# Two token groups computed together, weight block by weight block, at the start of a convolution and gated MLP kernel

## The chip, the cores and the metric

The kernel runs on one core of a Trainium2 chip. The metric is the device time of one execution in microseconds (us); lower is better. Engines are named as in the profile: PE is TensorE, DVE is VectorE, ACT is ScalarE, POOL is GpSimd, SP is the queue that issues the DMAs.

## The reference

`x` is 4 x 4096 x 192. A softmax over 7 taps per token and head gives weights, and each token becomes the weighted sum of itself and the six tokens before it, head by head (8 heads of 24 channels). The 16384 rows then go through a gated MLP with 1536 inner columns:

```python
w = softmax(weight_gen, axis=-1)                        # (B, S, 8, 7)
out = np.einsum('bshk,bskhg->bshg', w, x_unfolded)      # 7 taps
x = out.reshape(B * S, 192)
g = x @ w_gate                                          # 192 x 1536
silu = g * (1.0 / (1.0 + np.exp(-g)))
val = x @ w_val
y = (silu * val) @ w_out                                # 1536 x 192
```

The weights come as 64-bit floats; the kernel turns them into 32-bit ones itself.

## The kernel before

The 128 tiles of 128 tokens are worked on in 32 groups of four (`NG`, `JG`). Each group goes through 12 blocks of the inner dimension (`NF`); one group with one block is a step. A step is: the first half of the "up" products (`up_first`: 12 matmuls, the 64 left channels and the low rows of the 128 others), the second half (`up_second`: 6 matmuls), silu on ACT (`silu`), the product `hi` or `h` of silu and value on DVE (`gated`), and two steps later the "down" products with `w_out` (`down`), in four parts, three of them between the two halves of a step and one behind them (at a group's first block two and two).

Matmul operands are split into a high and a low part to keep precision: `x` and the up weights always; `h` and `w_out` too (`hi`, `lo`, `wo`), except in the first `PLAIN` groups, whose down products take plain 32-bit operands (`wo32`). A group that is split needs a `hi` copy on ACT and a `lo` subtraction on DVE in each step.

Two halves of a sum run in different rows of the array at once. That the second half does not overtake the first is kept by a relay: `told(ins)` puts an empty instruction on POOL that waits for a matmul, and `behind(ins, nop)` makes a later matmul wait for that instruction. It stands in POOL's queue in program order.

While group 0 runs, the weight blocks are converted (`weight_ops`), each in four pieces: `exponent` (DVE `e`, ACT `e` and `sign`, POOL `sign`), `mantissa_high` and `mantissa_low` (DVE `m` twice; the second also fetches the raw block four places ahead), and `value32` (DVE `w`, then ACT `wb_hi`, `wa_hi` and `wo`, POOL `wb_lo` and `wa_lo`). `wo32` is split into `wo` later (ACT and POOL).

The order of the work is written by hand. The loop at the end takes one step per pass; `todo[i]` holds the extra operations of step i, and `spread` lays a list evenly over some steps. In `gated`, `between()` takes one operation off that list. For a plain group all of them are issued ahead of `hi`; for the others one between `h` and `lo`, the rest behind.

The taps: group 0 has its seven products made by DVE one by one, copied in part by ACT, and added and turned by TensorE in one (`summed_turn`: 8 matmuls with the identity per tap, two `xatt` buffers). Group 1 has its products made by DVE and, three of them, by POOL (`aside`), added by DVE, and turned by 16 matmuls (`turn`). Later groups are added by DVE and turned by DVE and DMA (`turn_ops`). A group's taps are worked on during the steps of the group before.

Of the kernel before, what the change touches and what calls it, by code (L numbers as in the profile page):

```python
# [18 lines left out]
def dynconv_glu_kernel(  # L19
# [41 lines left out]
    LEAD1 = 1  # L61
    EXP1 = 16
    LOAD1 = 1
    WO = 9

    PLAIN = 1
    MOVED = 2

    HELPED = (0, 3)
    ASIDE = max(HELPED)  # L70
# [153 lines left out]
    def attention_ops(g):  # L224
        cx, cw = chunk_of(xcuts, g), chunk_of(wcuts, g)
        jx, jw = g * JG - xcuts[cx][0], g * JG - wcuts[cw][0]
        helped = HELPED[g] if g < len(HELPED) else 0
# [10 lines left out]
        if g == 0:  # L238
            return mul
# [12 lines left out]
        def aside(k):  # L252
            def go():
                tmp[k] = att.tile([P, JG, D], F32, tag="aside", name="aside", bufs=ASIDE)
                mul(nc.gpsimd, k, tmp[k])

            return go

        def add(k):
            def go():  # L260
                a = xatt[g][:, :, 0:D]
                nc.vector.tensor_tensor(out=a, in0=a, in1=tmp.pop(k), op=ALU.add)  # L262
                if g < MOVED and k == last:
                    a = xatt[g]
                    nc.scalar.activation(out=a[:, :, D:], in_=a[:, :, P:D], func=AF.Copy)

            return go

        ops = [first, product(1)]
        for k in range(2, K - helped):  # L270
            ops += [product(k), add(k - 1)]
        ops += [add(k) for k in range(K - helped - 1, last + 1)]
        return [aside(k) for k in range(K - helped, K)], ops
# [15 lines left out]
    def summed_turn(mul):  # L289

        ps = [ps_up.tile([P, NC], F32, tag="up", name="tr") for _ in range(2)]

        def tap(k):
            def go():
                a = att.tile([P, JG, 2 * P], F32, tag="xatt", name="xatt")
                mul(nc.vector, k, a[:, :, 0:D])
                nc.scalar.activation(out=a[:, :, D:], in_=a[:, :, P:D], func=AF.Copy)
                for half in range(2):
                    for t in range(JG):
                        nc.tensor.matmul(  # L300
                            ps[half][:, t * P : (t + 1) * P],
                            a[:, t, half * P : (half + 1) * P],
                            ident,
                            start=(k == 0 and t == 0),
                            stop=(k == K - 1 and t == JG - 1),
                        )

            return go

        return ps, [tap(k) for k in range(K)]  # L310

    def turn(g, ps, nop):

        places = ((1, LOW), (0, HIGH)) if nop else ((0, LOW), (1, HIGH))
        made = [
            nc.tensor.transpose(
                ps[half][:, t * P + r.start : t * P + r.stop],
                xatt[g][r, t, half * P : (half + 1) * P],
                ident[r, r],
            )  # L320
            for t in range(JG)
            for half, r in places
        ]
        if nop:
            behind(made[0], nop)
            return None
        return told(made[-1])

# [3 lines left out]
    def turn_ops(g):  # L332
# [3 lines left out]
        def blocks():  # L336
            cut = att.tile([P, JG, D], F32, tag="aside", name="cut", bufs=ASIDE)
# [204 lines left out]

    def down(g, f, pair, second):

# [4 lines left out]
        if opens:  # L549
            for t in ts:  # L550
                acc[t] = ps_dn.tile([P, 2 * D], F32, tag=f"dn{t}", name=f"dn{t}")
        order = ts if (f + second) % 2 == 0 else ts[::-1]
        tiles = [(t, r, slice(t * P, (t + 1) * P)) for t, r in zip(order, (LOW, HIGH))]
        if lo is None:
            made = [
                nc.tensor.matmul(  # L556
                    acc[t][:, 0:D], hi[r, cs], wo32[r, f], start=opens, stop=closes
# [3 lines left out]
        else:  # L561
            made = [
                nc.tensor.matmul(  # L563
                    acc[t],
# [5 lines left out]
                for t, r, cs in tiles  # L570
            ] + [
                nc.tensor.matmul(  # L572
                    acc[t][:, 0:D], lo[r, cs], wo[r, f, 0], start=False, stop=closes
# [6 lines left out]
        behind(made[0], half_done.pop(pair))  # L580
        if f < NF - 1:
            return
# [3 lines left out]
        n = D if lo is None else 2 * D  # L586
        for t in ts:
            nc.scalar.activation(out=osb[:, t, 0:n], in_=acc[t][:, 0:n], func=AF.Copy)  # L588
# [3 lines left out]
        if lo is not None:  # L592
            a = osb[:, t0:t1]
            nc.vector.tensor_tensor(
                out=a[:, :, 0:D], in0=a[:, :, 0:D], in1=a[:, :, D:], op=ALU.add
            )
        if g < MOVED:
            nc.sync.dma_start(
                out=outr[:, g * JG + t0 : g * JG + t1], in_=osb[:, t0:t1, 0:D]
            )  # L600
            return
# [9 lines left out]
    turned = {}  # L611
# [7 lines left out]
    with tc.manual_schedule():  # L619
# [32 lines left out]
        later = after[3:]  # L652
        loads = load_x(1) + load_taps(1)
# [6 lines left out]
        todo[0] += later[:3]  # L660
        spread(loads, LOAD1, LOAD1 + 7)
        spread(later[3:], NF - LEAD2 - 2, NF - LEAD2)
        spread(
            [lambda f=f: split(wo[:, f, 0], wo[:, f, 1], wo32[:, f]) for f in range(NF)],
            WO,
            NF + LAG - 1,
        )
# [10 lines left out]
        for g in range(1, NG):  # L678
            s0 = (g - 1) * NF - {1: LEAD1, 2: LEAD2}.get(g, LEAD)
            c = first_x.get(g)  # L680
            if c and c + 1 < len(xcuts):
                todo.setdefault(s0, []).append(lambda c=c: load_x(c + 1)[0]())
            asides, rest = attention_ops(g)
            spread(asides, max(s0, 0), s0 + NF - 4)
            spread(rest, max(s0, 0), s0 + NF - 3)
            if g < MOVED:
                turned[s0 + NF - 2] = g
                continue
            moves, halves = turn_ops(g)
            at = s0 + NF - 3  # L690
# [3 lines left out]
        steps = [(g, f) for g in range(NG) for f in range(NF)]  # L694
        for i in range(len(steps) + LAG + 1):
            ops = todo.pop(i, [])
            to_turn = turned.get(i)
            if i < len(steps):
                g, f = steps[i]
                sums, nop = up_first(g, f)  # L700
                if i in exps:
                    exps[i]()
            late = []
            if i > LAG:
                late = [(*steps[i - LAG - 1], 1, True)]
            if i > LAG and not to_turn:
                down(*late.pop())
            if to_turn:
                ps = [ps_up.tile([P, NC], F32, tag="up", name="tr") for _ in range(2)]
                turned_nop = turn(to_turn, ps, None)  # L710
            if LAG <= i < len(steps) + LAG:
                s = steps[i - LAG]
                late += [(*s, 0, False), (*s, 1, False), (*s, 0, True)]
                if not to_turn:
                    down(*late.pop(0))
                    if s[1]:
                        down(*late.pop(0))
                    else:
                        late.reverse()
# [7 lines left out]
            if to_turn:  # L727
                turn(to_turn, ps, turned_nop)
# [8 lines left out]
            if to_turn:  # L737
                for op in split_ops(to_turn, ps):
                    op()
# [35 lines left out]
```

## Time and profile before

| | |
|---|---|
| median of 3 runs | 1312.7 us (1311.3 to 1313.1) |
| profiled execution, its own time | 1312.98 us |
| its span | 1311.2 us |
| mean granted TensorE clock | 0.990 |
| PE busy | 1270.9 us, 97% |
| DVE busy | 1023.8 us, 78% |
| ACT busy | 594.3 us, 45% |
| POOL busy | 61.2 us, 5% |

The span runs from the first to the last instruction of the program. The busy share is an average: POOL has all its work in the first 103 us, in which the weights are converted, and DVE and PE differ between that stretch and the rest.

### The profile page before, as it was taken

How to read it: one execution, taken by the hardware profiler on the slowest of the kernel's cores; microseconds unless marked ns; L12 is line 12 of the kernel's file. 1: busy time of each engine (PE TensorE's matmuls, PEld its weight loads, DVE VectorE, ACT ScalarE, POOL GpSimd, SP SyncE). 2: the span in 40 equal slices, each digit the busy share in tenths (PEclk: the TensorE clock that was granted, in tenths of full speed). 3: DMA queues.
4: the chain of work that ended last, by engine and by line, in shares of the span. 5: the costliest groups of instructions: out<-in, count | busy, mean ns of one | idle time of the engine just before them, and what ended most of it. 6: DMA issues, size and time to landing. Idle time of an engine off the chain costs nothing.

```text
span 1311.2 us, 31268 instructions
## 1 busy us (share of the span) xinstructions
PE 1270.9 (97%) x13184; PEld 1242.9 (95%) x13184; DVE 1023.8 (78%) x1413; ACT 594.3 (45%) x1049; POOL 61.2 (5%) x62
## 2 busy tenths in 40 slices
PE   5689999999999999999999999999999999999997
PEld 5578899999999999999999999999999999999997
DVE  6978888777887777788777788877778877777843
ACT  5444444454444445444444544444454444444443
POOL 4750000000000000000000000000000000000000
PEclk9789999999999999999999999999999999999999
DMA  6511121212112121211212111221211212111010
GB/s 175 153 47 40 48 72 42 71 42 84 43 33 84 29 84 42 76 33 51 84 29 84 42 36 61 59 71 42 84 41 26 72 39 74 42 42 39 17 40 13
DMA packets 64149, 74.88 MB, mean 57 GB/s; under 512 B 6924, under 2 KB 53516, under 8 KB 62216
## 3 DMA queue, kind: packets, MB, share of 16 engines
q1 hardware_dynamic: 64008, 72.89, 20.1%
q8 instruction: 103, 1.69, 0.5%
q14 instruction: 38, 0.31, 0.1%
HBM read 48.48 MB, written 24.38 MB: 56 GB/s over the span
## 4 chain that ended last, share of the span: by engine, by line
PE 87%; DVE 6%; ACT 2%; DMA 2%; issue 1%; SPq 0%; POOL 0%; ACTq 0%; DVEq 0%; POOLq 0%
PE up L511 23%; PE up L499 22%; PE dn L563 21%; PE up L502 18%; PE dn L572 2%; DVE h L533 1%; DMA xt<-in_x_dram 1%; DVE prod L234 1%; PE tr L300 1%; DVE lo L536 1%; PE dn L556 1%; ACT sg L519 1%; ACT L519 0%; ACT L186 0%; DMA raw<-in_moe_w_gate_dram 0%
## 5 line engine op out<-in xcount | busy, mean ns | idle before, releaser
L563 PE MATMUL dn<-wo,hi 64*128 64x384 f32 x2976 | 578.8, 344 | 0.8 <-ACT osb L588 0.4
L572 PE MATMUL dn<-wo,lo 64*128 64x192 f32 x2976 | 512.2, 249 | 0.3 <-DVE lo L536 0.3
L563 PEld LDWEIGHTS dn<-wo,hi 64*128 64x128 f32 x2976 | 477.4, 184 | 6.9 <-ACT osb L588 2.3
L572 PEld LDWEIGHTS dn<-wo,lo 64*128 64x128 f32 x2976 | 456.4, 186 | 1.8 <-DVE lo L536 0.5
L534 ACT ACTIVATE hi<-h 128x512 fp32r<-128x512 f32 x372 | 235.3, 633 | 377.7 <-DVE h L533 377.7
L533 DVE TENSOR_TENSOR h<-up,sg 128x512 f32<-128x512 f32 x372 | 256.0, 688 | 181.5 <-ACT sg L519 181.3
L519 ACT ACTIVATE sg<-up 128x512 f32<-128x512 f32 x384 | 228.5, 595 | 302.4 <-PE up L511 295.4
L536 DVE TENSOR_TENSOR lo<-h,hi 128x512 fp32r<-128x512 f32 x372 | 254.7, 685 | 83.1 <-ACT hi L534 83.1
L499 PE MATMUL up<-xhi,wb_hi 64*128 64x512 f32 x768 | 223.7, 418 | 8.1 <-DVE hi L528 5.9
L511 PE MATMUL up<-xhi,wa_hi 64*128 64x512 f32 x768 | 218.9, 419 | 10.5 <-POOLq L282 10.4
L499 PE MATMUL up<-xlo,wb_hi 64*128 64x512 f32 x768 | 211.5, 392 | 1.5 <-DVE xlo L384 1.5
L499 PE MATMUL up<-xhi,wb_lo 64*128 64x512 f32 x768 | 211.4, 394 | 0.0
L502 PE MATMUL up<-xhi,wa_hi 64*128 64x512 f32 x768 | 209.9, 391 | 0.2 <-ACT xhi L377 0.2
L502 PE MATMUL up<-xhi,wa_lo 64*128 64x512 f32 x768 | 209.6, 390 | 0.0
L502 PE MATMUL up<-xlo,wa_hi 64*128 64x512 f32 x768 | 208.8, 388 | 0.3 <-DVE xlo L384 0.3
L511 PE MATMUL up<-xhi,wa_lo 64*128 64x512 f32 x768 | 208.2, 391 | 0.0
L511 PE MATMUL up<-xlo,wa_hi 64*128 64x512 f32 x768 | 207.4, 389 | 0.0
L234 DVE TENSOR_TENSOR prod<-xt,wt 128x768 f32<-128x768 f32 x183 | 176.0, 962 | 0.2
L262 DVE TENSOR_TENSOR xatt<-xatt,prod 128x768 f32<-128x768 f32 x183 | 176.1, 962 | 0.0
L499 PEld LDWEIGHTS up<-xhi,wb_hi 64*128 64x128 f32 x768 | 128.6, 185 | 13.0 <-DVE hi L528 7.4
L511 PEld LDWEIGHTS up<-xhi,wa_hi 64*128 64x128 f32 x768 | 127.2, 185 | 13.1 <-POOLq L282 13.1
L502 PEld LDWEIGHTS up<-xhi,wa_hi 64*128 64x128 f32 x768 | 128.4, 185 | 3.1 <-ACT xhi L377 0.7
(60 smaller groups left out, 1306.0 us busy)
## 6 DMA issues: line engine op xcount, KB each, us to landing
xt<-in_x_dram SPq DMA_DIRECT2D x14, 1344.0 KB, 6.8
turned<-cut SPq DMA_DIRECT2D x120, 96.0 KB, 2.0
out_dram<-osb SPq DMA_DIRECT2D x116, 96.0 KB, 1.9
t<-turned SPq DMA_DIRECT2D x60, 128.0 KB, 2.6
t<-turned SPq DMA_DIRECT2D x30, 256.0 KB, 3.0
raw<-in_moe_w_out_dram SPq DMA_DIRECT2D x12, 192.0 KB, 2.7
wt<-in_weight_gen_dram SPq DMA_DIRECT2D x3, 672.0 KB, 4.4
raw<-in_moe_w_gate_dram SPq DMA_DIRECT2D x12, 128.0 KB, 2.2
```

Of the source, the lines that this page charges most:

```text
L234: engine.tensor_tensor(out=into.rearrange("p t (h i) -> p t h i", h=H), in0=src, in1=w, op=ALU.mult)
L262: nc.vector.tensor_tensor(out=a, in0=a, in1=tmp.pop(k), op=ALU.add)
L300: nc.tensor.matmul(ps[half][:, t * P : (t + 1) * P], a[:, t, half * P : (half + 1) * P], ident, start=(k == 0 and t == 0), stop=(k == K - ...
L499: nc.tensor.matmul(ps, w[r, fs], m[r], start=(n == 0), stop=False)
L502: ins = nc.tensor.matmul(sums[i], w[r, i, fs], m[r], start=False, stop=False)
L511: ins = nc.tensor.matmul(sums[i], w[r, i, fs], m[r], start=False, stop=(n == len(full) - 1))
L519: nc.scalar.activation(out=sg, in_=sums[0], func=AF.Silu)
L533: nc.vector.tensor_tensor(out=h, in0=sums[1], in1=sg, op=ALU.mult)
L534: nc.scalar.activation(out=hi, in_=h, func=AF.Copy)
L536: nc.vector.tensor_tensor(out=lo, in0=h, in1=hi.bitcast(F32), op=ALU.subtract)
L563: nc.tensor.matmul(acc[t], hi[r, cs], wo[r, f].rearrange("p a d -> p (a d)"), start=opens, stop=False,)
L572: nc.tensor.matmul(acc[t][:, 0:D], lo[r, cs], wo[r, f, 0], start=False, stop=closes)
```

## The change

Groups 0 and 1 are both plain now (`PLAIN = 2`) and are computed together. A list `steps` gives the order: four steps of group 0 (`HEAD`), then in turn one of group 1 and one of group 0, four blocks ahead, and at the end four of group 1. Each weight block is therefore used by two groups while the conversion goes on, and its pieces are laid by the step in which group 0 needs it (`due`). In the first four steps all extra operations stand ahead of `hi`; in the other plain steps one does and the rest stand behind.

Group 1's taps are made like those of group 0, by `summed_turn`, during steps 0 to 3, in the two PSUM banks that group 1's down products take later. The POOL products, the sums on DVE and `turn` are gone. The down sums of a plain group take two banks, two tiles in each, and are copied out by two ACT instructions. The softmax of the first taps stands wholly ahead of step 0. Group 2's taps begin at step 5. The splits of `wo32` follow group 0's blocks, the first six of them at step 10.

```diff
-    PLAIN = 1
+    PLAIN = 2
     MOVED = 2
+    HEAD = 4
...
-        if g == 0:
+        if g < MOVED:
             return mul
...
+        if g == 0:
+            ps = [ps_up.tile([P, NC], F32, tag="up", name="tr") for _ in range(2)]
+        else:
+            ps = [ps_dn.tile([P, NC], F32, tag=f"dn{2 + n}", name=f"tr{n}") for n in range(2)]
...
         if g < PLAIN:
-            while between():
+            while between() and g == 0 and f < HEAD:
                 pass
...
+            if pair == 0:
+                behind(made[0], half_done.pop(0))
+                behind(made[0], half_done.pop(1))
...
-        for op in after[:3]:
+        for op in after[:6]:
             op()
-        ps, taps = summed_turn(attention_ops(0))
+        ps, taps = summed_turn(0)
         meanwhile = w0 + w1[:2]
-        for op in taps[:2]:
+        for op in taps[:2] + after[6:]:
             op()
...
+        steps = [(0, f) for f in range(HEAD)]
+        for f in range(NF - HEAD):
+            steps += [(1, f), (0, f + HEAD)]
+        steps += [(1, f) for f in range(NF - HEAD, NF)]
+        steps += [(g, f) for g in range(2, NG) for f in range(NF)]
...
-        for i in range(NF):
-            ops = todo.setdefault(i, [])
-            for f, part in ((i + 2, 3), (i + 3, 1), (i + 4, 0), (i + 3, 2)):
-                if f < NF:
-                    ops.append(convert[f][part])
+        ps1, taps1 = summed_turn(1)
+        due = [steps.index((0, f)) for f in range(NF)]
+        for f in range(2, NF):
+            for part, ahead in ((3, 2), (1, 3), (0, 4), (2, 3)):
+                if (f, part) not in ((2, 1), (2, 2), (2, 0), (3, 0)):
+                    todo.setdefault(max(due[f] - ahead, 0), []).append(convert[f][part])
+        spread(taps1, 0, HEAD - 1)
+        spread(split_ops(1, ps1), HEAD - 1, HEAD)
+        spread(load_x(1) + load_taps(1), LOAD1, LOAD1 + 7)
+        for f in range(NF):
+            todo.setdefault(max(due[f] + 3, HEAD + 6), []).append(
+                lambda f=f: split(wo[:, f, 0], wo[:, f, 1], wo32[:, f])
+            )
...
-        for g in range(1, NG):
-            s0 = (g - 1) * NF - {1: LEAD1, 2: LEAD2}.get(g, LEAD)
+        for g in range(2, NG):
+            s0 = (g - 1) * NF - (LEAD if g > 2 else NF - HEAD - 1)
```

How it moves instructions, at the three places that the prediction speaks of. First PE, behind the first step (`up` is what a step writes, `tr` the tap sums, `xatt` a tap). Before, the second half of step 0 is followed by step 1:

```order
L511 MATMUL up<-xhi,wa_hi 128x512 x2
L511 MATMUL up<-xlo,wa_hi 128x512 x2
L511 MATMUL up<-xhi,wa_lo 128x512 x2
L499 MATMUL up<-xhi,wb_hi 128x512 x2
L499 MATMUL up<-xlo,wb_hi 128x512 x2
L499 MATMUL up<-xhi,wb_lo 128x512 x2
```

Now three taps of group 1 stand between them (two rows each), and two more behind each of steps 1 and 2:

```order
L483 MATMUL up<-xhi,wa_hi 128x512 x2
L483 MATMUL up<-xlo,wa_hi 128x512 x2
L483 MATMUL up<-xhi,wa_lo 128x512 x2
L289 MATMUL tr_307<-ident,xatt 128x128 x4
L289 MATMUL tr_308<-ident,xatt 128x128 x4
L289 MATMUL tr_307<-ident,xatt 128x128 x4
L289 MATMUL tr_308<-ident,xatt 128x128 x4
L289 MATMUL tr_307<-ident,xatt 128x128 x4
L289 MATMUL tr_308<-ident,xatt 128x128 x4
L471 MATMUL up<-xhi,wb_hi 128x512 x2
```

PE's queue is in order, so step 1 stands behind the third tap. Second ACT, in steps 0 to 2 (`sg` is silu, `xatt` the copy that a tap needs). Before:

```order
L519 ACTIVATE sg<-up 128x512
L412 ACTIVATE wb_hi<-w 128x128
L412 ACTIVATE wa_hi<-w 128x2x128
L476 ACTIVATE wo_95<-w 128x192
L431 ACTIVATE e<-e,exp_bias 128x576
L433 ACTIVATE sign<-raw 128x576
L519 ACTIVATE sg<-up 128x512
```

Now:

```order
L286 ACTIVATE xatt<-xatt 128x4x64 x3
L491 ACTIVATE sg<-up 128x512
L384 ACTIVATE wb_hi<-w 128x128
L384 ACTIVATE wa_hi<-w 128x2x128
L448 ACTIVATE wo_95<-w 128x192
L403 ACTIVATE e<-e,exp_bias 128x576
L405 ACTIVATE sign<-raw 128x576
L286 ACTIVATE xatt<-xatt 128x4x64 x2
L491 ACTIVATE sg<-up 128x512
L286 ACTIVATE xatt<-xatt 128x4x64 x2
```

The copies of the fourth and fifth tap stand behind silu of step 1 and the five pieces of a weight block. Third DVE, a step in the middle of the conversion (`hi` is the product of the step; `e`, `m` and `w` are pieces of weight blocks). Before, all pieces stand ahead of `hi`:

```order
L462 SCALAR_TENSOR_TENSOR w<-m,sign 128x576
L439 TENSOR_SCALAR m<-raw 128x576
L422 TENSOR_SCALAR e<-raw 128x576
L449 SCALAR_TENSOR_TENSOR m<-raw,m 128x576
L262 TENSOR_TENSOR xatt<-xatt,aside 128x4x192
L528 TENSOR_TENSOR hi<-up,sg 128x512
```

Now, over an odd and an even step:

```order
L434 SCALAR_TENSOR_TENSOR w<-m,sign 128x576
L500 TENSOR_TENSOR hi<-up,sg 128x512
L394 TENSOR_SCALAR e<-raw 128x576
L251 TENSOR_TENSOR xatt<-xatt,prod 128x4x192
L411 TENSOR_SCALAR m<-raw 128x576
L500 TENSOR_TENSOR hi<-up,sg 128x512
L421 SCALAR_TENSOR_TENSOR m<-raw,m 128x576
L230 TENSOR_TENSOR prod<-xt,wt 128x768
```

One conversion is spread over two steps, and `e` stands behind the odd step's `hi`.

## Rows read from the trace of the kernel before

**Rows 1.** Busy time by stretches; columns as in the first line.

```profile
core 0: us, PE busy (x) PEld busy (x) DVE busy (x) ACT busy (x) POOL busy (x), PEclk, DMA share, GB/s
70.00:80.00 10.00, 6.58 (x55) 4.88 (x54) 9.93 (x14) 5.04 (x11) 6.47 (x6) 1.00 0.02 5
80.00:90.00 10.00, 8.67 (x71) 8.19 (x68) 7.28 (x11) 3.90 (x12) 4.70 (x7) 0.66 0.00 0
```

**Rows 2.** Timeline of PE, group 2: start, duration, instruction, [pause before it].

```profile
150.84 0.41 PE L499 MATMUL up<-xhi,wb_hi 64*128 64x512 f32 x1
...
154.07 0.41 PE L499 MATMUL up<-xhi,wb_hi 64*128 64x512 f32 x1
```

**Rows 3.** Waits of PE, 0 to 120 us: total, times, longest.

```profile
PE up L511 <- POOLq L282: 10.4, 7, 3.7
```

**Rows 4.** Timeline of PE: end of step 0, and two pauses.

```profile
29.66 0.40 PE L511 MATMUL up<-xhi,wa_lo 64*128 64x512 f32 x2
...
76.37 0.50 PE L511 MATMUL up<-xhi,wa_hi 64*128 64x512 f32 x2 [1.05 <-POOLq L282]
...
82.19 0.58 PE L316 MATMUL tr<-ident,xatt 64*128 64x64 f32 x6 [1.33 <-DVE hi L528]
```

**Rows 5.** Timeline of POOL.

```profile
76.31 1.42 POOL L434 TENSOR_TENSOR sign<-sign,e 128x576 f32<-128x576 f32 x1
...
99.96 1.41 POOL L413 TENSOR_TENSOR wo<-wo,wo 128x192 fp32r<-128x192 f32 x2 [3.06 <-PE dn L556]
```

**Rows 6.** Timeline of PE, a plain step: first half, second half, down, next step.

```profile
90.83 0.53 PE L499 MATMUL up<-xhi,wb_hi 64*128 64x512 f32 x1
...
93.19 0.52 PE L511 MATMUL up<-xhi,wa_hi 64*128 64x512 f32 x1
...
94.01 0.48 PE L556 MATMUL dn<-wo,hi 64*128 64x192 f32 x3
...
94.20 0.52 PE L499 MATMUL up<-xhi,wb_hi 64*128 64x512 f32 x1
```

**Rows 7.** Timeline of DVE.

```profile
31.63 0.75 DVE L449 SCALAR_TENSOR_TENSOR m<-raw,m 128x576 int32<-128x576 int32 x1
32.30 0.38 DVE L191 TENSOR_REDUCE sm<-wt 128x32 f32<-128x224 f32 x1
...
35.02 2.05 DVE L234 TENSOR_TENSOR xatt<-xt,wt 128x768 f32<-128x768 f32 x1
...
71.97 0.68 DVE L528 TENSOR_TENSOR hi<-up,sg 128x512 f32<-128x512 f32 x1
72.57 1.37 DVE L462 SCALAR_TENSOR_TENSOR w<-m,sign 128x576 f32<-128x576 int32 x1
...
74.24 0.45 DVE L422 TENSOR_SCALAR e<-raw 128x576 int32<-128x576 int32 x1
...
89.12 0.95 DVE L234 TENSOR_TENSOR prod<-xt,wt 128x768 f32<-128x768 f32 x1
...
94.90 0.69 DVE L528 TENSOR_TENSOR hi<-up,sg 128x512 f32<-128x512 f32 x1 [0.33 <-ACT sg L519]
```

**Rows 8.** Timeline of ACT.

```profile
9.56 0.42 ACT L297 ACTIVATE xatt<-xatt 128x256 f32<-128x256 f32 x1 [1.94 <-DVE xatt L234]
...
24.88 0.60 ACT L377 ACTIVATE xhi<-tr 128x512 fp32r<-128x512 f32 x1 [0.30 <-PE tr L300]
...
45.56 0.31 ACT L412 ACTIVATE wb_hi<-w 128x128 fp32r<-128x128 f32 x1 [0.52 <-DVE w L462]
...
47.04 0.71 ACT L433 ACTIVATE sign<-raw 128x576 f32<-128x576 int32 x1
```

**Rows 9.** Chain that ended last: start, length; taps of group 0, 16 records each.

```profile
9.67 3.68 PE tr L300 x16
...
15.64 5.64 PE tr L300 x48
```

**Rows 10.** The chain again, about the exponentials of the next softmax.

```profile
110.16 1.11 ACT L186
...
114.10 0.61 ACT sg L519
```

More of the change, by code (lines that the diff above doesn't have):

```diff
@@ L310, in summed_turn @@
         return ps, [tap(k) for k in range(K)]
[L312 to L327, printed above, removed]
     Q = 32
@@ L541, in dynconv_glu_kernel, with opened @@
     half_done = {}
+    banks = {}
+    def opened(g):
+        for n in range(2):
+            bank = ps_dn.tile([P, 2, D], F32, tag=f"dn{2 * g + n}", name=f"dn{2 * g + n}")
+            banks[g, n] = bank
+            for t in (n, n + 2):
+                acc[g, t] = bank[:, t // 2]
     def down(g, f, pair, second):
@@ L548, in down @@
         ts = (2 * pair, 2 * pair + 1)
-        if opens:
+        if opens and pair == 0 and lo is None:
+            opened(g)
+        elif opens and lo is not None:
             for t in ts:
-                acc[t] = ps_dn.tile([P, 2 * D], F32, tag=f"dn{t}", name=f"dn{t}")
+                acc[g, t] = ps_dn.tile([P, 2 * D], F32, tag=f"dn{t}", name=f"dn{t}")
         order = ts if (f + second) % 2 == 0 else ts[::-1]
@@ L556, in down @@
                 nc.tensor.matmul(
-                    acc[t][:, 0:D], hi[r, cs], wo32[r, f], start=opens, stop=closes
+                    acc[g, t],
+                    hi[r, cs],
+                    wo32[r, f],
+                    start=opens and pair == 0,
+                    stop=closes and pair == 1,
                 )
@@ L579, in down @@
             return
-        behind(made[0], half_done.pop(pair))
-        if f < NF - 1:
+        if lo is None:
+            if pair == 0:
+                behind(made[0], half_done.pop(0))
+                behind(made[0], half_done.pop(1))
+        else:
+            behind(made[0], half_done.pop(pair))
+        if f < NF - 1:
+            return
+        if lo is None:
+            if pair:
+                osb = outp.tile([P, JG, 2 * D], F32, tag="osb", name="osb", bufs=1)
+                for n in range(2):
+                    nc.scalar.activation(
+                        out=osb[:, n::2, 0:D], in_=banks[g, n], func=AF.Copy
+                    )
+                nc.sync.dma_start(out=outr[:, g * JG : (g + 1) * JG], in_=osb[:, :, 0:D])
             return
@@ L585, in down @@
         osb = osb_t[g]
-        n = D if lo is None else 2 * D
         for t in ts:
-            nc.scalar.activation(out=osb[:, t, 0:n], in_=acc[t][:, 0:n], func=AF.Copy)
+            nc.scalar.activation(out=osb[:, t], in_=acc[g, t], func=AF.Copy)
         if g < NG - 1 and pair == 0:
@@ L591, in down @@
         t0, t1 = (ts[0] if g == NG - 1 else 0), ts[1] + 1
[L592 to L601, printed above, removed]
+        a = osb[:, t0:t1]
+        nc.vector.tensor_tensor(
+            out=a[:, :, 0:D], in0=a[:, :, 0:D], in1=a[:, :, D:], op=ALU.add
+        )
         blocks = outr.rearrange("(j c) t d -> c j t d", c=Q)
@@ L702, in dynconv_glu_kernel @@
                     exps[i]()
+            if i > LAG:
+                down(*steps[i - LAG - 1], 1, True)
             late = []
[L704 to L710, printed above, removed]
             if LAG <= i < len(steps) + LAG:
                 s = steps[i - LAG]
[L713 to L719, printed above, removed]
+                down(*s, 0, False)
+                late = [(*s, 0, True)]
+                if s[1] or s[0] < PLAIN:
+                    down(*s, 1, False)
+                else:
+                    late.append((*s, 1, False))
             if i < len(steps):
```

58 lines of the change are left out of this document (11 added, 47 removed).

## The prediction

> **What bounds the kernel now.** I first read busy time and granted clock by stretches of 10 us, which show where TensorE is not full: 6.58 of 10 us from 70 to 80 [rows 1]. Later it is: in the timeline of TensorE two steps of group 2 follow each other 3.23 us apart (154.07 less 150.84, [rows 2]), matmul on matmul. What can be won or lost lies in the stretch before, while the weights are still being converted. There I read TensorE's waits: it stood 10.4 us, 7 times, at the second half of a step for a word from POOL's sequencer [rows 3]. This is the relay in told() and behind(): a wait in POOL's queue that passes on the end of TensorE's first half. It stands behind whatever POOL was given before it. The reader sees it at 76.37: TensorE goes on 0.06 us after POOL's sign product started at 76.31 [rows 4, 5]. So a sign product that waits for ScalarE holds TensorE too. It is its start that counts, not its end: that product runs 1.42 us and TensorE did not wait for it.
>
> Then the timing inside a plain step [rows 6, 7]: steps start 3.37 us apart (94.20 less 90.83), the second half starts 2.36 after the step does, its six matmuls take 0.82, and VectorE's product hi follows 4.07 after the start, so silu ends about 1.7 after the second half began. A plain step needs 3.37 where a split one needs 3.23.
>
> All steps are counted as in the list of the change: 0 to 3 are group 0 alone, 4 to 19 alternate, 20 to 23 end group 1. Before, step 28 (fifth step of group 2) starts at 150.84 and everything behind it runs at the even pace. I place the same step in the change; the difference is my forecast.
>
> **Up to the first step: nothing.** Two softmax pieces move ahead. The first falls into VectorE's wait for x, the second delays a conversion whose result is needed 5 us later, while the third tap waits for TensorE in any case. The bounds are -0.4 and +0.4; I take 0.
>
> **The head, steps 0 to 3.** TensorE ends step 0 at 30.06 (29.66 + 0.40, [rows 4]). Now seven taps of group 1 stand in its queue between the steps, three behind step 0. The softmax pieces that began at 32.30 [rows 7] are gone from there and so is one e (0.45 with its overlap), so the first tap's product starts at about 31.9. Alone a product took 0.95, beside POOL's work 2.05 [rows 7]; I take the lower value, since POOL's sign starts just behind it. With ScalarE's copy of 0.42 [rows 8] TensorE gets the tap at 33.4 (34.5 by the other end).
>
> A tap costs TensorE 1.88 (three in 5.64), but the first of group 0 took 3.68 [rows 9]. After pauses TensorE is put at the lower of its two levels, 1.2 GHz: in the stretch from 80 to 90 us, with a pause of 1.33 at 82.19, the granted clock averaged 0.66, so 6.8 us ran at half, a loss of at most 3.4 [rows 1, 4]. I price the first tap behind a pause of over 3 us at 3.68, the rest at 1.88. Three taps: 33.4 to 40.9. Step 1 has no down parts: 1.4 for its first half (an estimate, somewhat under twice 0.82), second half from 42.3, silu done at 44.0.
>
> Here the new order costs. On ScalarE the copies of taps 3 and 4 stand behind silu of step 1 and behind wb_hi, wa_hi, wo, e and sign of the next block. Those five took 2.19 (45.56 to 47.75, [rows 8]). So the copy ends at 46.6, and TensorE has stood 3.4. Taps 3 and 4: 3.68 + 1.88, to 52.2. Step 2: 1.4 + 0.6 for half of the down parts (2.36 less 1.4 is three quarters of them), silu done at 55.9, copy, taps 5 and 6 from 56.3 to 60.1. Step 3: second half from 62.5, silu done at 64.2, the five ScalarE pieces to 66.4, and two xhi of under 0.60 each [rows 8] to 67.5. Only then can step 4, the first of group 1, start; TensorE has stood about 4 us again. I add 0.3 for xlo and 2.0 for the lower clock (bounds 0 and 3.4). Step 5 starts at 67.5 + 3.4 + 2.3 = 73.2.
>
> **Steps 4 to 23.** Nineteen steps from 5 to 24 at 3.37 are 64.0, and two steps now share one converted block, so VectorE alone need not bound them. But before, all conversions of a step ran ahead of hi; now e stands behind hi, in the odd steps 5 to 15. Counted from such a step's start: hi starts at 4.07 and takes 0.60 (71.97 to 72.57), then e, whose start lies 2.07 ahead of POOL's sign (74.24 to 76.31) [rows 5, 7]. So the relay is let through at 4.07 + 0.60 + 2.07 + 0.06 = 6.80. TensorE wants it at 3.37 + 2.36 = 5.73. That is a pause of 1.07 in each pair, six times: **6.4 us**. Pauses of 1.05 left the granted clock at 1.00 (70 to 80 us, [rows 1]), so I add nothing for that.
>
> Smaller terms: at step 10 six wo splits come at once. The relay passes with the sixth copy on ScalarE, in time, but POOL works about 0.7 on each (1.41 for two, [rows 5]) beside three VectorE operations with two SBUF operands, and hi of step 11 comes late: 0.8 (0 to 1.3). Softmax in steps 12 to 15 makes hi late twice: 0.5 together (0 to 2). The exponentials at step 16 take ScalarE away for 3.9 (110.16 to 114.10, [rows 10]); two steps of slack cover most: 0.8 (0 to 3.9). Sum 2.1.
>
> On the other side, twelve lo subtractions and hi copies of group 1, six sums and three POOL products are gone; POOL, ScalarE and VectorE are then free around step 24, and the banks of group 0 are long copied out when group 2 opens its own. So I give the four split steps 24 to 27 no pause: 4 x 3.23 = 12.9. That group 1's twelve steps are plain now costs 12 x (3.37 - 3.23) = 1.7, which is in the 3.37. The DMAs are the same ones in another order; raw blocks are fetched 8 steps ahead of use and x for group 2 several steps ahead, so I cost them at nothing; if that cover went, an e would come late and hold the relay.
>
> **Sum.** Step 28 starts at 73.2 + 64.0 + 6.4 + 2.1 + 12.9 = 158.6, against 150.84: 7.8 us later. The profiled execution took 1312.98; so 1320.8, and 0.3 less against the median of 1312.7: **1320.5**. The case's own range, from the bounds above, is 1315 to 1325.
>
> **Rivals.** (1) *The relay costs nothing.* If e came early enough, or TensorE got to the second half 1.07 later anyway, the 6.4 go, and with them the 1.3 by which a late hi acts through it: 1312.8, no change. The point of decision is sign's start 5.73 after an odd step's start. For it: the relay only minds starts. Against it: the 7 waits of [rows 3].
> (2) *That, and the clock stays up in the head.* The two taps and step 4 then save 1.8 + 1.8 + 2.0: 1307. For it: one TensorE pause of 1.05 did no harm; against it, the new ones are three times as long.
> (3) *VectorE becomes the bound between steps 4 and 16, held by POOL.* A product beside POOL's work took 2.05 in place of 0.95 [rows 7]. Behind hi of an even step, which ends at 6.80 + 1.71 + 0.60 = 9.1, stand m (0.75 with its overlap, [rows 7]), a product (0.95) and w (like m): 11.5, and the next hi is due at 11.9. If the three lost 0.5 each, that hi would come 1.1 late: six pairs, 6 us more, 1326.5. The Trainium skill, SBUF — State Buffer, section "Who interferes with whom", says that a VectorE instruction with two SBUF inputs and a GpSimd instruction that reads SBUF exclude each other, the second waiting out the first. By that rule the time would be that of this rival wherever POOL's work lies beside the three; the trace agrees with the block (2.05 for 0.95). Against it: sign is over (6.75 + 1.42 = 8.17) before hi of the even step (8.5) and the three behind it, so I give it 0.12.
> (4) *The clock falls in the 1.07 pauses*, as after 1.33 at 82.19. Two falls at up to 3.4: 1327.
>
> **Chances.** Forecast 0.50, rivals 0.17, 0.13, 0.12 and 0.08. A measurement tells about 0.2% (2.6 us) from no change. Faster: rival 2 and a third of rival 1, 0.18. Same: the rest of rival 1 and the low end of the forecast, 0.16. Slower: 0.66. The range 1309 to 1327 leaves out most of rival 2 and the tail above.
>
> **What would show it.** Right: step 4's first matmul near 67.5; TensorE's waits for POOL's sequencer six times near 1.1 us in steps 6 to 16; three pauses over 3 us between 30 and 68 us with the clock at the lower level behind them; step 28 near 159. Wrong: step 28 before 151, or the pauses in steps 6 to 16 ended by something else, or none.

## The result and the profile after

The changed kernel takes **1321.1 us** (median of 4 runs, 1319.3 to 1322.2), the kernel before 1312.9 (4 runs, 1311.3 to 1313.3). The ratio is 1.0064, with a 95% interval of 1.0046 to 1.0081: 8.2 us slower. The profiled execution took 1320.99 us with a span of 1319.2. The forecast was 1320.5.

Busy time alone would not say so. On the page after, DVE has 1006.8 us where it had 1023.8, and POOL 49.9 where it had 61.2. PE has 1284.0 where it had 1270.9: it took over group 1's sums. The loss lies in the first 130 us, by stretches [rows 1]. First a stretch of the kernel before that was not shown:

```profile
60.00:70.00 10.00, 6.99 (x64) 5.59 (x62) 10.00 (x12) 4.38 (x11) 7.82 (x7) 1.00 0.83 276
```

And the same view after the change:

```profile
core 0: us, PE busy (x) PEld busy (x) DVE busy (x) ACT busy (x) POOL busy (x), PEclk, DMA share, GB/s
40.00:50.00 10.00, 7.94 (x51) 6.59 (x50) 4.15 (x5) 3.25 (x8) 2.81 (x3) 0.85 0.17 48
60.00:70.00 10.00, 6.57 (x38) 5.11 (x36) 2.25 (x4) 3.60 (x8) 2.55 (x3) 0.70 0.01 2
70.00:80.00 10.00, 9.20 (x86) 8.02 (x86) 7.12 (x9) 3.95 (x8) 3.32 (x3) 0.96 0.34 102
90.00:110.00 20.00, 16.66 (x164) 13.99 (x160) 16.41 (x21) 11.10 (x27) 13.49 (x15) 1.00 0.28 97
```

DVE was full before. Now, between 60 and 70 us, neither DVE (2.25 of 10) nor PE (6.57) is: they wait for each other and for ACT (3.60). What is lost while no engine is full is lost in waits, and so in the order of the queues; here a lower granted clock (0.70) comes on top. What PE waited for from 0 to 170 us (total, times, longest) stands against [rows 3]:

```profile
PE tr L289 <- DVE xatt L230: 10.6, 2, 9.4
PE up L483 <- POOLq L267: 8.1, 7, 1.6
PE up L471 <- ACT xhi L349: 4.1, 2, 3.4
PE tr L289 <- ACT xatt L286: 1.9, 1, 1.9
PE up L471 <- DVE xlo L356: 1.5, 1, 1.5
```

The 9.4 of the first line is group 0's first tap, ahead of step 0; 0.7 of the third line and the 1.5 of the last belong to step 0 too, and the kernel before waits as long there (0.69 and 1.52). The rest are the two places of the prediction: the head (1.25, 1.95 and 3.39) and the relay (seven pauses; their 8.1 us are less than the 10.4 before). The timeline of PE has them, and the start of step 28 at 158.47, against 150.84 [rows 2], 7.6 us later:

```profile
32.26 1.01 PE L289 MATMUL tr<-ident,xatt 128*128 128x128 f32 x3 [1.25 <-DVE xatt L230]
45.74 1.62 PE L289 MATMUL tr<-ident,xatt 128*128 128x128 f32 x11 [1.95 <-ACT xatt L286]
64.28 0.79 PE L471 MATMUL up<-xhi,wb_hi 64*128 64x512 f32 x2 [3.39 <-ACT xhi L349]
77.75 0.50 PE L483 MATMUL up<-xhi,wa_hi 64*128 64x512 f32 x2 [0.80 <-POOLq L267]
102.01 0.50 PE L483 MATMUL up<-xhi,wa_hi 64*128 64x512 f32 x2 [1.55 <-POOLq L267]
123.79 0.50 PE L483 MATMUL up<-xhi,wa_hi 64*128 64x512 f32 x2 [1.04 <-POOLq L267]
158.47 0.41 PE L471 MATMUL up<-xhi,wb_hi 64*128 64x512 f32 x2
```

POOL's timeline shows what let the relay through at 77.75 and 123.79. An instruction of POOL starts 0.06 and 0.04 us earlier, as at 76.31 before [rows 4, 5]. The second row is the six `wo` splits, the third a `sign` that belongs to the pause at 102.01:

```profile
77.69 1.92 POOL L406 TENSOR_TENSOR sign<-sign,e 128x576 f32<-128x576 f32 x1 [1.05 <-ACT sign L405]
...
95.44 5.33 POOL L385 TENSOR_TENSOR wo<-wo,wo 128x192 fp32r<-128x192 f32 x6 [0.63 <-ACT wo L384]
...
102.78 1.42 POOL L406 TENSOR_TENSOR sign<-sign,e 128x576 f32<-128x576 f32 x1
...
123.75 0.60 POOL L385 TENSOR_TENSOR wo<-wo,wo 128x192 fp32r<-128x192 f32 x1 [2.92 <-ACT wo L384]
```

ACT leads there. Its `sign` of 76.83 ends at 77.54, and PE goes on 0.21 us later; that of 101.10 ends at 101.81, and PE goes on 0.20 later. The pause at 45.74 ends behind the copies of 45.28, the one at 64.28 behind the `xhi` of 63.15, the one at 123.79 behind the exponentials:

```profile
45.28 0.71 ACT L286 ACTIVATE xatt<-xatt 128x256 f32<-128x256 f32 x2
...
63.15 1.08 ACT L349 ACTIVATE xhi<-tr 128x512 fp32r<-128x512 f32 x2
...
76.15 0.78 ACT L403 ACTIVATE e<-e,exp_bias 128x576 int32<-128x576 int32 x1 [0.43 <-DVE e L394]
76.83 0.71 ACT L405 ACTIVATE sign<-raw 128x576 f32<-128x576 int32 x1
...
101.10 0.71 ACT L405 ACTIVATE sign<-raw 128x576 f32<-128x576 int32 x1
...
118.89 1.28 ACT L183 ACT_TABLE_LOAD   x1
120.19 1.33 ACT L183 ACTIVATE wt<-wt 128x1344 f32<-128x1344 f32 x1
121.53 1.28 ACT L491 ACT_TABLE_LOAD   x1
122.83 0.60 ACT L491 ACTIVATE sg<-up 128x512 f32<-128x512 f32 x1
123.32 0.35 ACT L384 ACTIVATE wo<-wo 128x192 fp32r<-128x192 f32 x1
```

And ahead of ACT stands DVE, whose `e` comes behind the odd step's `hi`, in step 5 and in step 11:

```profile
74.99 0.69 DVE L500 TENSOR_TENSOR hi<-up,sg 128x512 f32<-128x512 f32 x1 [1.22 <-ACT sg L491]
75.60 0.45 DVE L394 TENSOR_SCALAR e<-raw 128x576 int32<-128x576 int32 x1
...
95.75 0.90 DVE L421 SCALAR_TENSOR_TENSOR m<-raw,m 128x576 int32<-128x576 int32 x1
96.58 1.34 DVE L230 TENSOR_TENSOR prod<-xt,wt 128x768 f32<-128x768 f32 x1
97.85 1.15 DVE L434 SCALAR_TENSOR_TENSOR w<-m,sign 128x576 f32<-128x576 int32 x1
98.92 0.68 DVE L500 TENSOR_TENSOR hi<-up,sg 128x512 f32<-128x512 f32 x1
99.52 0.80 DVE L394 TENSOR_SCALAR e<-raw 128x576 int32<-128x576 int32 x1
```

In the second five rows, beside the six `wo` splits, `hi` starts 0.4 late (98.92 for 94.44 + 4.07) and `e` takes 0.80 in place of 0.45. So the pause at 102.01 is 1.55 and not 0.80.

### The profile page after: what moved, and what is told of

Read it like the earlier page. It is cut to its first block, busy times and chain, and to the rows that moved or that the text cites. A ratio compares the mean times of both kernels' runs of the same rounds, so it can differ in the third digit from the quotient of the medians.

```text
span 1319.2 us, 31481 instructions
## 1 busy us (share of the span) xinstructions
PE 1284.0 (97%) x13280; PEld 1233.0 (93%) x13280; DVE 1006.8 (76%) x1397; ACT 589.6 (45%) x1039; POOL 49.9 (4%) x59
## 4 chain that ended last, share of the span: by engine, by line
PE 89%; DVE 5%; ACT 3%; issue 2%; DMA 1%; POOL 0%; SPq 0%; ACTq 0%; DVEq 0%; POOLq 0%
PE up L483 22%; PE up L471 22%; PE dn L550 19%; PE up L474 18%; PE dn L559 3%; PE tr L289 2%; PE dn L539 1%; DVE h L505 1%; DVE prod L230 1%; ACT sg L491 1%; DVE lo L508 0%; DVE xatt L230 0%; ACT L491 0%; ACT L183 0%; DVE m L421 0%
## 5 line engine op out<-in xcount | busy, mean ns | idle before, releaser
L550 PE MATMUL dn<-wo,hi 64*128 64x384 f32 x2880 | 553.9, 344 | 0.4 <-ACT hi L506 0.4
L559 PE MATMUL dn<-wo,lo 64*128 64x192 f32 x2880 | 487.8, 249 | 0.3 <-DVE lo L508 0.3
L550 PEld LDWEIGHTS dn<-wo,hi 64*128 64x128 f32 x2880 | 449.2, 184 | 11.0 <-ACT osb L588 1.4
L559 PEld LDWEIGHTS dn<-wo,lo 64*128 64x128 f32 x2880 | 428.6, 186 | 4.5 <-DVE lo L508 0.5
L505 DVE TENSOR_TENSOR h<-up,sg 128x512 f32<-128x512 f32 x360 | 248.0, 689 | 179.4 <-ACT sg L491 179.2
L508 DVE TENSOR_TENSOR lo<-h,hi 128x512 fp32r<-128x512 f32 x360 | 246.6, 685 | 80.4 <-ACT hi L506 80.4
L483 PE MATMUL up<-xhi,wa_hi 64*128 64x512 f32 x768 | 214.7, 421 | 8.3 <-POOLq L267 8.1
L474 PE MATMUL up<-xhi,wa_hi 64*128 64x512 f32 x768 | 203.4, 391 | 0.0
L474 PE MATMUL up<-xhi,wa_lo 64*128 64x512 f32 x768 | 203.4, 391 | 0.0
L483 PE MATMUL up<-xhi,wa_lo 64*128 64x512 f32 x768 | 202.8, 390 | 0.0
L474 PE MATMUL up<-xlo,wa_hi 64*128 64x512 f32 x768 | 202.4, 388 | 0.0
L483 PE MATMUL up<-xlo,wa_hi 64*128 64x512 f32 x768 | 202.0, 388 | 0.0
L483 PEld LDWEIGHTS up<-xhi,wa_hi 64*128 64x128 f32 x768 | 121.8, 185 | 11.7 <-POOLq L267 11.6
L474 PEld LDWEIGHTS up<-xhi,wa_hi 64*128 64x128 f32 x768 | 122.0, 185 | 5.6
```

What stands on the lines that cost most here:

```text
L474: ins = nc.tensor.matmul(sums[i], w[r, i, fs], m[r], start=False, stop=False)
L483: ins = nc.tensor.matmul(sums[i], w[r, i, fs], m[r], start=False, stop=(n == len(full) - 1))
L505: nc.vector.tensor_tensor(out=h, in0=sums[1], in1=sg, op=ALU.mult)
L508: nc.vector.tensor_tensor(out=lo, in0=h, in1=hi.bitcast(F32), op=ALU.subtract)
L550: nc.tensor.matmul(acc[g, t], hi[r, cs], wo[r, f].rearrange("p a d -> p (a d)"), start=opens, stop=False,)
L559: nc.tensor.matmul(acc[g, t][:, 0:D], lo[r, cs], wo[r, f, 0], start=False, stop=closes)
```

## The experiments

**Theory**: the loss is two losses in two places. In the head, ACT and DVE serve a step's conversion before the taps that TensorE's queue needs first; behind it, the relay waits for a late `e`. Both are matters of order. **Rivals**: the taps on TensorE or the plain products are dear in themselves, or the taking of turns is. All edits are to the changed kernel unless said otherwise. Where an edit acts is told by the us between the starts of steps, from TensorE's timelines. The starts of steps 0, 5 and 24 in the kernel before:

```profile
25.53 0.50 PE L499 MATMUL up<-xhi,wb_hi 64*128 64x512 f32 x2 [0.69 <-ACT xhi L377]
...
56.37 0.88 PE L499 MATMUL up<-xhi,wb_hi 64*128 64x512 f32 x2
...
135.35 0.42 PE L499 MATMUL up<-xhi,wb_hi 64*128 64x512 f32 x1
```

And in the change:

```profile
24.73 0.50 PE L471 MATMUL up<-xhi,wb_hi 64*128 64x512 f32 x2 [0.69 <-ACT xhi L349]
...
70.93 0.53 PE L471 MATMUL up<-xhi,wb_hi 64*128 64x512 f32 x2
...
145.13 0.53 PE L471 MATMUL up<-xhi,wb_hi 64*128 64x512 f32 x2
```

Two things are not in the table: step 0 starts between 24.4 and 26.1, and from step 24 to 28 the kernel before takes 15.5, those in which TensorE turns group 1's taps 13.3 or 13.4.

| kernel | 0 to 5 | 5 to 24 | time, ratio to before (95%) |
|---|---|---|---|
| before | 30.8 | 79.0 | 1312.9 |
| the change | 46.2 | 74.2 | 1321.1, 1.0064 (1.0046 to 1.0081) |
| two ahead of hi | 43.6 | 71.0 | 1316.5, 1.0042 (1.0027 to 1.0057) |
| pause filled | 42.3 | 74.2 | 1318.0, 1.0049 (1.0034 to 1.0064) |
| taps first | 36.0 | 74.2 | 1311.5, 0.9996 (0.9986 to 1.0006) |
| both | 36.1 | 71.0 | 1308.8, 0.9976 (0.9967 to 0.9985) |
| taps first, ahead of silu | 37.4 | 76.1 | 1314.3, 1.0020 (1.0011 to 1.0030) |
| no turns | 42.3 | 83.4 | 1326.1, 1.0103 (1.0083 to 1.0123) |
| no turns, taps first | 29.1 | 73.7 | 1305.5, 0.9954 (0.9939 to 0.9969) |
| no turns, taps in 3 steps | 42.4 | 68.5 | 1311.7, 0.9993 (0.9983 to 1.0002) |

Against the kernel before, the change loses 15.4 in the head, where it also does more, and takes 4.8 less from step 5 to 24. So the loss itself lies in the head; the late `e` is a gain that was not taken.

**1. Two operations ahead of `hi`.** `e` moves ahead of the odd step's `hi` (and the second `m` ahead of the even step's).

```diff
             while between() and g == 0 and f < HEAD:
                 pass
+            if not (g == 0 and f < HEAD):
+                between()
```

> The changed kernel, but behind the head two operations, not one, stand ahead of hi, so that e of the next weight block comes before hi of an odd step. Theory (the relay behind POOL's sign product holds TensorE): the seven waits for POOL's sequencer, 8.1 us in the changed kernel, fall under 2 us, step 28 comes near 151 in place of 158.5, and the time is 1312 to 1316. Rival (the loss is the added TensorE work, seven taps and plain down products): the waits turn into other waits and the time stays at 1320 to 1322. Rival (VectorE is the bound in steps 6 to 17): hi comes later by one e each time and the time stays or grows to 1323.

1316.5, just above the range of the theory; its waits under 2 us and its step 28 near 151 did not come (5.1 and 153.2). PE's waits, same view as above:

```profile
PE up L483 <- POOLq L267: 5.1, 7, 1.7
PE up L471 <- ACT xhi L349: 4.1, 2, 3.4
```

The relay's waits fall from 8.1 to 5.1 and steps 5 to 24 take 3.2 less; the ratio fell by 0.0022, 2.9 us. (The median is 4.6 lower. The head, which this edit leaves alone, took 2.6 less in the profiled execution, by the clock: the stretches from 40 to 50 and from 60 to 70 were granted 1.00 and 0.83 for 0.85 and 0.70. The first of them:

```profile
40.00:50.00 10.00, 7.95 (x64) 6.33 (x64) 4.81 (x6) 3.24 (x8) 2.81 (x3) 1.00 0.14 42
```

The intervals of the two ratios overlap; the 3.2 us of steps 5 to 24, and the same 3.2 in experiment 4, are the better evidence.) So the place of these pieces costs about 3 us. Of what is left, most stands on ACT: `e` and `sign` behind silu and the three `w` pieces.

**2. The pause ahead of step 4 filled** with eight matmuls that add zero, to price the clock apart from the pause.

```diff
             for what in late:
                 down(*what)
+            if i == HEAD - 1:
+                for n in range(8):
+                    nc.tensor.matmul(acc[0, n % 2], none, wo32[:, 0], start=False, stop=False)
```

> The changed kernel with eight more matmuls on TensorE behind step 3, which add zeros to group 0's down sums and fill 2.6 us of the 3.39 us pause ahead of step 4. Theory (that pause lowers the clock, and the lower clock costs 2 to 3.4 us): the clock stays at the upper level from 60 to 71 us, step 4 starts where it did, step 5 two to three us earlier, and the time is 1318 to 1319.5. Rival (the clock there fell for another reason, or what it costs is hidden): the time stays at 1321 or grows.

1318.0, as expected; the intervals of its ratio and the change's overlap, so the trace has to show what the edit did. The stretch around step 4:

```profile
60.00:70.00 10.00, 9.06 (x78) 7.78 (x78) 3.94 (x7) 4.09 (x9) 2.56 (x3) 1.00 0.01 2
```

The granted clock is 1.00 there, not 0.70, and step 4 takes 3.95 us (63.55 to 67.50) and not 6.65 (64.28 to 70.93). Against that execution the matmuls that did nothing bought 2.7 us: the clock behind the pause, at its lower level of 1.2 GHz, cost nearly as much as the pause of 3.39. It varies: in the run of experiment 1, behind the same 3.39, step 4 took 5.59, against 3.95 a cost of 1.6. (The other 1.2 in the head is again the clock between 40 and 50.)

**3. Taps first.** In the head the taps and the split stand ahead of the weight pieces of their step.

```diff
-        todo[0] = [w2[1], w3[0], w2[2]]
         ps1, taps1 = summed_turn(1)
+        spread(taps1, 0, HEAD - 1)
+        spread(split_ops(1, ps1), HEAD - 1, HEAD)
+        todo.setdefault(0, []).extend([w2[1], w3[0], w2[2]])
...
-        spread(taps1, 0, HEAD - 1)
-        spread(split_ops(1, ps1), HEAD - 1, HEAD)
```

> The changed kernel, but in the head the taps of group 1 and the split of their sum stand ahead of the weight conversions of the same step. Theory (the head's pauses come from ScalarE's order): the pauses of 1.25, 1.95 and 3.39 us at 32.3, 45.7 and 64.3 shrink to about 0, 0.5 and 1.2, step 4 comes near 60 in place of 64.3, less of the stretch from 60 to 71 runs at the lower clock, and the time is 1312 to 1317. Rival (the head is bound by VectorE and the two tap buffers): step 4 stays within 1 us of 64.3 and the time at 1320 to 1322.

1311.5, better than expected and no different from before. The steps 0 to 5 take 10.2 us less, the steps 5 to 24 exactly as long as in the change: the two places are independent. The pause ahead of step 4 is 1.37, the clock falls in the head once (about 29 to 32 us) and not three times. About 4 of the 10.2 us are pauses (1.26 and 1.37 for 1.25, 1.95 and 3.39); most of the rest, by the granted clock, is matmuls at the lower level.

**4. Both, and further.** Experiments 1 and 3 together; then, with taps first, the two operations ahead of silu as well:

```diff
-            while between() and g == 0 and f < HEAD:
+            while g == 0 and f < HEAD and between():
...
                 up_second(g, f, sums, nop)
+                if g < PLAIN and (g or f >= HEAD):
+                    for op in ops[:2]:
+                        op()
+                    ops = ops[2:]
                 sg = silu(sums)
```

> The taps and the split of group 1 stand ahead of the weight pieces in the head, and two operations stand ahead of hi in the plain steps behind it. Theory: the head's pauses and the relay's pauses are two losses that lie in different stretches, so the gains add. The first edit alone gave 1311.5 (9.6 us under the change), the second alone 4.6 under it, so 1306 to 1308; TensorE's waits for POOL's sequencer, 8.7 us with the first edit alone, fall by about 3 to under 6. Rival: VectorE has used up its slack once the head is short (the conversion as a whole then sets the end), and the second edit gives nothing more: 1310.5 to 1312.5, with the same pauses ended by something else.

> As the run before, but the two operations are issued ahead of silu as well, so that ScalarE's e and sign of a block stand ahead of silu in its queue and not behind it and behind wb_hi, wa_hi and wo. Theory: what TensorE still waits for behind the relay is ScalarE's late sign; with it early the waits for POOL's sequencer go below 2.5 us and the time to 1303 to 1306. Rival: the e that silu now stands behind is made by VectorE late in the step, silu and hi come later by it and the relay's pause becomes a pause for silu or for the bank: 1308 or more, waits of the second half for POOL's sequencer small, others of the step's first half for the silu or hi of a step before.

Both: 1308.8, a little above the 1306 to 1308 expected, waits for the relay 5.7. The gains add: steps 0 to 5 take 36.1 (36.0 with the one alone), steps 5 to 24 take 71.0, as with the other alone. Ahead of silu: 1314.3, the rival's time, though it had these waits small and others in their place. They did not go (8.7 with taps first alone):

```profile
PE up L483 <- POOLq L267: 8.3, 7, 2.1
```

In step 11 ACT stood 3.78 for DVE's `w` and then had its pieces, `e` and `sign` ahead of silu: at 91.93 silu started as the `sign` of 91.33 ended, and DVE waited 1.99 for it. The pair of steps 6 and 7 takes 6.7 us for 7.8 with taps first alone, but the pairs from step 12 on take 9.4, 9.0 and 12.1 for 8.6, 8.6 and 9.8.

**5. The relay on SP**, out of POOL's queue, for the plain groups; in the change, and with taps first:

```diff
-    def told(ins):
+    def told(ins, g):
...
-        nop = nc.gpsimd.nop()
+        nop = (nc.sync if g < PLAIN else nc.gpsimd).nop()
```

> The changed kernel with the relay of the plain groups in SP's queue in place of POOL's; POOL keeps all its products. Theory (TensorE's waits in steps 6 to 17 come from the relay's place behind POOL's sign): the 8.1 us of waits for POOL's sequencer go, SP's take under 1 us of their place, step 28 comes near 150.5 and the time is 1312 to 1315. Rival (SP's queue holds the relay as well, behind loads that wait for a buffer): waits for SP's sequencer of 5 us and more, 1317 to 1325. Rival (hi itself is late, so the second half would be held later anyway): the waits move to the first half of the step after next and the time is 1317 to 1321.

> Both: taps and split ahead of the conversions in the head (measured alone: 1311.5), and the relay of the plain groups in SP's queue. Theory (the two losses are separate and add up): 1311.5 less 7 to 8.5, 1302.5 to 1305, clear of the kernel before (1312.2). Rival (what one gives back the other takes, since VectorE or the first conversions then bound steps 4 to 17): 1308 to 1312.

1340.3 (1.0208, 1.0188 to 1.0229) and 1331.9 (1.0155, 1.0140 to 1.0171): missed by far. The first is the rival of SP's queue, beyond its 1325; the second lies outside both of its ranges. Waits of PE, then of SP's queue, in the first of the two:

```profile
PE up L483 <- SPq L267: 14.0, 4, 5.4
...
SPq L380 <- DVE m L421: 8.6, 3, 2.9
SPq L324 <- DVE cut L313: 8.4, 1, 8.4
```

SP's queue holds weight loads that wait for DVE's `m` to free a raw block, and group 2's turn that waits for `cut`; the relay stands behind these. Fewer pauses, but of 2.65 to 5.40, and the granted clock fell behind each. A relay is as good as the worst wait that stands ahead of it in its queue.

**6. No turns**: group 0 runs through alone (`HEAD = 12`), its taps' pieces one by one over steps 0 to 10; then the same with taps first.

```diff
-    HEAD = 4
+    HEAD = 12
...
-            todo.setdefault(max(due[f] + 3, HEAD + 6), []).append(
+            todo.setdefault(max(due[f] + 3, 10), []).append(
...
-            s0 = (g - 1) * NF - (LEAD if g > 2 else NF - HEAD - 1)
+            s0 = (g - 1) * NF - (LEAD if g > 2 else 3)
```

> The changed kernel with HEAD = 12: group 0 first, then group 1, not in turn; the taps of group 1 on TensorE over all twelve steps, the first wo splits still at step 10, group 2's taps from step 9. Theory (what the change lost lies in the pauses of the head and of the steps in turn, not in the plain products or in the taps on TensorE): steps 0 to 11 take about 4.6 us each, all conversions again ahead of hi, so the relay is let through early; step 28 comes between 137 and 146 and the time is 1299 to 1308, under both kernels. Rival (the work put on TensorE is what costs): step 28 near 158 or later, 1320 or more. Rival (VectorE bounds one block per step as in the kernel before): steps 0 to 11 take 5.5 us each and the time is 1310 to 1315.

> HEAD = 12 (no turns) as in the run before, with the taps and the split ahead of the conversions of the same step. There TensorE waited 22.7 us for taps and its clock fell six times. Theory (a tap in TensorE's queue costs by where its product stands on VectorE and ScalarE): most of those waits go, step 12 comes near 95 in place of 108 and the time is 1309 to 1316. Rival (with one group per block VectorE bounds the first twelve steps in any case): step 12 stays over 103 and the time over 1320; the turns of two groups are then what the change gains by.

The first missed: 1326.1. With the taps behind the pieces of every step TensorE waited for them time after time:

```profile
PE tr L289 <- DVE xatt L230: 15.9, 4, 9.5
PE tr L289 <- ACT xatt L286: 6.8, 5, 1.9
```

The second is the best kernel of the study, **1305.5**, 0.46% (0.31 to 0.61%) under the kernel before and better than expected (step 12 at 88.0 for about 95). Its stretches:

```profile
50.00:60.00 10.00, 10.00 (x96) 8.72 (x94) 9.79 (x13) 5.82 (x14) 5.64 (x7) 1.00 0.59 173
60.00:70.00 10.00, 9.72 (x90) 8.32 (x88) 9.93 (x11) 5.99 (x14) 7.69 (x7) 1.00 0.16 56
```

DVE and PE are both full: the taps fill what TensorE has free while DVE converts, and the relay costs 2.3 us in all.

**7. No turns, taps in steps 0 to 2**, since the run with taps first and turns (1311.5) and this best one differ in two things. Against the best one:

```diff
-        spread(taps1, 0, HEAD - 1)
-        spread(split_ops(1, ps1), HEAD - 1, HEAD)
+        spread(taps1, 0, 3)
+        spread(split_ops(1, ps1), 3, 4)
```

> The run with taps first and the turns kept gave 1311.5, the one with taps first and no turns 1305.5; but they differ in two things, the turns and the place of group 1's seven taps (steps 0 to 2 there, steps 0 to 10 here). This run has no turns and the taps in steps 0 to 2. Theory: the turns are what costs, since each pair pays the relay for an e behind hi, and without them the conversion is over by step 12 with TensorE free behind it: 1304 to 1307, waits for POOL's sequencer under 4 us. Rival: the turns cost nothing, and the gain is that TensorE adds the taps in the stretch that VectorE bounds anyway, where they are hidden; then this run is as slow as with turns: 1310 to 1313, step 12 near 88 and the steps 4 to 12 bound by VectorE or the relay.

1311.7, the rival's time (its step 12 came at 95.5, not near 88). The stretches:

```profile
50.00:60.00 10.00, 10.00 (x96) 9.13 (x94) 3.20 (x6) 4.35 (x11) 2.55 (x3) 1.00 0.47 154
60.00:70.00 10.00, 6.07 (x40) 4.97 (x38) 9.86 (x14) 5.41 (x13) 5.07 (x5) 0.71 0.37 107
```

With the taps crowded into three steps first TensorE is full and DVE idle (3.20 of 10), then the conversion is behind, DVE is full, and TensorE stands 3.93 us at the relay, after which the clock falls. Against the run with turns, steps 0 to 5 take 6.3 more and steps 5 to 24 5.7 less. So, with the taps in three steps, the turns alone are worth about nothing: they move the pauses. Without turns the crowding costs 6.2 us by the medians (1311.7 less 1305.5), 5 by the ratios. Turns with the taps spread were not run.

**8. Plain products alone**: the kernel before with `PLAIN = 2`.

```diff
-    PLAIN = 1
+    PLAIN = 2
```

> The kernel before with PLAIN = 2 and nothing else: group 1's down products are plain and its hi copies and lo subtractions are gone; its taps, the order of steps and the relay are those of before. Theory (the plain products alone cost TensorE 1.7 us and give back part of the 2.7 us of pauses in steps 22 to 28): 1310.5 to 1313.5, no change. Rival (VectorE's relief is what steps 12 to 28 need): 1307 to 1310. Rival (all extra operations ahead of hi in group 1's steps make hi late): 1314 to 1318.

1309.2 (0.9984, 0.9975 to 0.9994), the rival: 2 us are gained, though TensorE's plain steps take 0.14 more each. So plain products are not dear either; that DVE, which was full, has the `lo` subtractions less would explain the gain, but was not tried apart.

By ratios to before, in us of 1312: plain products -2; with group 1's taps summed and turned by TensorE, well placed, -6; these crowded into three steps -1; in turns the same; and behind the weight pieces +8. The order in the head lost what the parts had gained.

## Why the prediction held, point by point

The sum held (step 28 at 158.5, forecast 158.6), but its parts were off in opposite ways: step 5 came 2.3 early, and from there to step 28 it took 2.1 more than forecast. That these cancel is luck. The causes were foreseen: the new waits lie in the head and at the relay, and, but for the first, the pieces named ended them. Of the signs of being right, step 28 near 159 came, and so did the six relay pauses in steps 6 to 16 (0.80 to 1.55, for near 1.1); step 4 near 67.5 did not, and of the three pauses over 3 us in the head one came.

**Up to the first step.** 24.73 against about 25.5, outside the bounds of 0.4. Kernels with the same code up to there started step 0 between 24.4 and 26.1, so this is the scatter of a single execution, which I had not allowed for.

**The head.** The pauses were shorter than forecast. The first was 1.25 for 3.3, the second 1.95 for 3.4, and the one behind step 2 did not come at all; ahead of step 4 it was 3.39 for about 4. The step that failed is "So the copy ends at 46.6, and TensorE has stood 3.4": it makes the whole tap wait for ACT's copy, as does the 33.4 for the first tap (whose terms, besides, add up to 33.3). Only the matmuls of the second half of the channels need that copy. Those of the first half went ahead of it: at 32.26, behind DVE's product alone, while the copy started at 33.58, and from 42.64 to 43.8, in the gap. With that, and step 0 being 0.8 earlier, step 4 started at 64.3 for 67.5. It took 6.65 for 3.37, 3.3 more, where I had added 2.3 for `xlo` and the clock; with the pause filled it took 3.95, so `xlo` cost 0.6 and the clock 2.7. Step 5: 70.9 for 73.2.

**Steps 5 to 24.** 74.2 for 72.5. Without a relay pause the pitch is 3.35 (70.93 to 74.28; forecast 3.37). The first three relayed steps took 4.45, 4.53 and 4.45, that is 1.08, 1.16 and 1.08 over the forecast pitch, for a forecast 1.07: this term was right in its cause and its size. (The waits of PE give only 0.80 for the same pauses, because matmuls start closer together than they last; a pause is better read as a difference of step starts.) The later ones were larger: 1.83, 1.81 and 1.79, and a seventh, 1.32, in step 17. Of the smaller terms 3.5 came for a forecast 2.1, all through the relay. The six `wo` splits gave 0.76 (forecast 0.8). The softmax gave 0.74 and 0.72 (forecast 0.5 in all): each time `hi` started 0.5 late and `e` took 0.67 for 0.45. The exponentials gave the 1.32 (forecast 0.8): silu of step 16 started 3.9 later for them, the `wo` copy stood behind it, and POOL's split of that copy held the relay.

**Steps 24 to 28** took 13.3 for 12.9.

**Rivals.** *The relay costs nothing*: false, it costs 10 us of pitch (the seven excesses above), 3 of which came back by one move of `e`. *The clock stays up in the head*: false; three falls in the profiled execution. *VectorE held by POOL*: the Trainium skill, SBUF — State Buffer, section "Who interferes with whom", has VectorE instructions with two SBUF inputs and GpSimd's reads exclude each other. The rows agree: beside the six splits `m` took 0.90, the product 1.34 and `w` 1.15, for 0.75, 0.95 and 0.75 [rows 7]. The 0.9 that this makes came once, not in six pairs, because elsewhere `sign` was over ahead of these three, as argued. The same section says that `tensor_scalar` can take the shared ports too; `e`, of that kind, took 0.80 and not 0.45, and the first `m`, of that kind too, 1.68 for 0.45 beside the `sign` of 77.69. The prediction had not counted this, and for `e` it is half of the 0.76. *The clock falls in the relay's pauses*: false; from 80 us on it was 1.00, through pauses of up to 1.55.

## What to carry to other kernels

When work moves to the engine that bounds a kernel, ask what serves it: the same seven taps left the kernel 6 us faster than before where they were spread over steps in which VectorE was the bound, and 8 us slower where they were crowded into three steps and their products and copies queued behind pieces that were due later. Put the piece that an in-order queue needs next ahead of those. An empty instruction that passes on a signal should stand in a queue where nothing ahead of it can wait; if none is free, move forward what it stands behind.

## What was not expected of the hardware

A pause costs twice when the granted clock falls behind it: 3.39 of waiting ahead of step 4 and 2.7 of slow matmuls in that execution, which eight matmuls that add zero bought back. Which pauses do so was not plain from their length. Behind 1.95 at 45.74 the clock fell, but behind the same pause, 1.94 long, it stayed at 1.00 in the runs of experiments 1 and 2, in which TensorE's order up to there is the change's. So the clock's part in one execution is no fixed price of the code. It was at its lower level about the pauses of 1.52 and 1.25 between 26 and 33 us, too; relay pauses of 1.55, 1.53 and 1.50 left it at 1.00. What else decides it was not tried.

The relay on POOL waits neither for the end nor for the start of the work ahead of it, but for what that work waits for. At 77.75 POOL's `sign` had just started (77.69) and ran on for 1.92 us. At 102.01 POOL was still busy with a `wa_lo` and its `sign` started only at 102.78, yet PE went on, 0.20 us after ACT's `sign` had ended; in the runs of experiments 1 to 3 and in the first of 4 the same step shows the same (0.21 each). In the forecast I took the start for the condition [rows 4, 5]; it gave the right number only because the two coincide when POOL is free.
